# fp16 parts and a bound in place of fp32r in a feed-forward layer, with sums of squares for maxima

## The chip, the cores and the metric

The kernel runs on one core of one Trainium2 chip. The core has TensorE (PE, with its weight loads shown as PEld), VectorE (DVE), ScalarE (ACT), GpSimd (POOL) and SyncE (SP, which issues most DMAs). The metric is device time in microseconds (us); lower is better. A profile is one further execution, recorded by the hardware profiler.

## What is computed

Attention over 4 batches, 12 heads, 448 positions, head size 64, with a mix of the heads before and after the softmax; its output is 1792 tokens of 768 values. Then two feed-forward layers:

```python
def _moe_ref(x, w_in, w_out):            # layer 0: d_ff 2048
    h = x @ w_in
    g = h * np.cos(h)
    return g @ w_out
def _moe2_ref(x, w_gate, w_val, w_out):  # layer 1: d_ff 1536
    g = x @ w_gate
    silu = g * (1.0 / (1.0 + np.exp(-g)))
    val = x @ w_val
    return silu * val @ w_out
```

The attention inputs are fp32; the weights `w_in`, `w_out`, `w_gate`, `w_val` and `w_out2` reach the kernel as fp64 words, of which it makes fp32 bits itself.

## The kernel before

**Order of the work.** Attention comes first (functions of `attention`, planned block by block, 180 blocks); during its last chunk `early_plan` places the first work of layer 0 among its blocks, at s plus a number, s being the first block of the last chunk. Then `run` and `steps` write out the order of the rest by hand: a list of steps (layer, group g of 256 hidden columns, token block t of 448 tokens), 8 groups x 4 blocks in layer 0 and 6 x 4 in layer 1. Step i does the first product (`l1`, L737 to L739) of entry i in two halves e, and the second product (`l2`, L840 to L842) of entry i - 1, output by output (m from 0 to 5). Each engine takes its instructions strictly in the order in which they are issued, so this order is the schedule.

**Precision by parts.** An operand is split into a high and a low part, and three matmuls (high x high, high x low, low x high) stand for one in fp32. The first products of both layers use fp16 parts, with the weights scaled by a power of two, found from their maxima. In layer 0 the second product uses parts in fp32r, both for the activation (`hidden_b`, L783 and L784) and for `w_out`, which therefore needs no scale; in layer 1 it uses fp16 parts: `hidden_b`, `hidden_c` and `hidden_d` find the maximum of each activation block (L775) and scale by it.

**One step of layer 0.** PE: 36 matmuls of the first product and 36 of the second, each 128 x 128 weights by 448 columns. DVE per half: L759 and L760 (the angle of the cosine), then, after ACT's Sin (L761), L771, the product with the hidden value. ACT casts it to the high part, POOL subtracts for the low part. For each of the six outputs DVE adds the PSUM result to the accumulator in SBUF (`l2`, L850; group 0 is a copy by ACT, L846). The second product has three PSUM banks, the first four.

**Weights.** `load_next` issues the DMA of one raw half slab (384 KB) from SP into one of 8 buffers (`RAWS`). `w_max` (L517, DVE) takes the maximum of a half; `w_sum` (L526 to L531) joins those of a batch and makes a power of two; `w_sum_all` (L539) is a matmul with ones over the partitions; `w_unit` (L547, L548) gives the scale and its inverse. A half is converted by `w_shift` (ACT, L559), three bit operations (`w_bits`, L567, L569, L573, DVE), and `w_split` (ACT cast L597, POOL subtraction L598); `w_by` (L608) makes the product of the scales. `w_steps` lists this work: three items for a conversion (one for each bit operation, with what belongs to it), one item for a maximum; the maxima of a batch are put ahead of the conversion before. `fill(n)` takes the next n items, where their room (the earliest step) is reached and no sum is pending. In a step of layer 0 the calls are: `fill(3)` before the first half, one after its angle, one after its product, and three during the second product.

**From layer 0 to layer 1.** In the last group each finished output of `l2` gets a maximum by DVE (L854), six for a token block; `next_max` and `next_unit` make a scale of them; `next_part` writes layer 1's input parts: for the last three outputs and for block 0, ACT scales (L884) and casts (L885) and POOL subtracts (L886).

Of the kernel before, what the change touches and what calls it, by code (L numbers as in the profile page):

```python
# [46 lines left out]
RAWS = 8  # L47
# [3 lines left out]
def f(ap):  # L51
    return ap.bitcast(F32)
# [386 lines left out]
class FeedForward:  # L439


    def __init__(self, ctx, tc, xs, w_in, w_out, w_gate, w_val, w_out2, outT):
        self.ctx, self.tc, self.xs, self.outT = ctx, tc, xs, outT
        self.X, self.raw, self.part, self.G, self.W, self.PH = {}, {}, {}, {}, {}, {}
        self.n_ps = self.n_wi = 0
# [5 lines left out]
        self.unit = [self.p_const.tile([128, 4], F32, name=f"unit{layer}") for layer in range(2)]  # L451
        self.scale, self.by = {}, {}
        self.hm = {}
# [11 lines left out]
    def open_early(self):  # L465
        self.p_wr = self.pool("m_wr", RAWS, side="right")
# [14 lines left out]
    def open_late(self):  # L481
        self.p_wo = self.pool("m_wo", 4)
        self.p_wi.append(self.pool("m_wi1", WI - 2))
# [28 lines left out]
    def w_max(self, key, z):  # L512


        u, i = self.scale[key]
# [5 lines left out]
    def w_sum(self, batch):  # L521

        nc = self.tc.nc
        u = self.scale[batch[0]][0]
        m = u[:, 2]
        nc.vector.tensor_tensor(m, u[:, 0], u[:, 1], op=ALU.max)  # L526
        if batch[0][1] == "o":
            nc.vector.tensor_tensor(m[:, 0:1], m[:, 0:1], m[:, 1:2], op=ALU.max)
            nc.vector.tensor_copy(m[:, 1:2], m[:, 0:1])
        nc.vector.tensor_scalar(m, m, 2.0 ** -112, None, op0=ALU.mult)  # L530
        nc.vector.tensor_scalar(  # L531
            m.bitcast(I32), m.bitcast(I32), 3, 0x7C000000, op0=ALU.logical_shift_left, op1=ALU.bitwise_and
        )

    def w_sum_all(self, batch):

        ps = self.part["sum", batch[0]] = self.ps_sum("su_" + self.nm(batch[0], 0))
        m = self.scale[batch[0]][0][:, 2].bitcast(BF16)[:, 1::2]
        self.tc.nc.tensor.matmul(ps[:, 0:2], self.ones, m, start=True, stop=True)  # L539

    def w_unit(self, batch):
# [3 lines left out]
        u = self.scale[batch[0]][0].bitcast(I32)  # L545
        ps = self.part.pop(("sum", batch[0]))[:, 0:2].bitcast(I32)
        nc.vector.tensor_scalar(u[:, 3], ps, 0x7C000000, None, op0=ALU.bitwise_and)  # L547
        nc.vector.tensor_scalar(  # L548
            u[:, 4], u[:, 3], 3, 31 << 23, op0=ALU.logical_shift_right, op1=ALU.bitwise_xor
        )  # L550

    def w_shift(self, key, z):
# [4 lines left out]
        t = self.p_wr.tile([128, 3, 128], F32, tag="f", bufs=2, name="f_" + self.nm(key, z))  # L557
        by = self.one(key, 4) if key in self.scale else 2.0 ** -112
        nc.scalar.activation(t, top, AF.Copy, scale=by)  # L559
# [18 lines left out]
    def one(self, key, row):  # L578
        u, i = self.scale[key]
        return u[:, row, i:i + 1]  # L580

    def w_split(self, key, z):
        nc = self.tc.nc
        first, half = key[1] == "i", key in self.scale
# [478 lines left out]
```

## Time and profile before

| | |
|---|---|
| median of 3 runs | 1395.35 us (1393.73 to 1397.68) |
| profiled execution | 1398.5 us, span on the core 1396.7 us |
| PE busy | 1366.9 us (98%), 9580 matmuls |
| PE weight loads | 883.6 us (63%) |
| DVE busy | 1050.7 us (75%), 2416 instructions |
| ACT busy | 649.2 us (46%) |
| POOL busy | 444.8 us (32%) |
| HBM read and written | 75.45 and 10.37 MB |

Layer 0 runs from about 430 to 915 us of the span, layer 1 from there to the end. A row of a group (by line) has the line, engine and operation, output and input tiles, shapes, count; then busy us and the mean ns of one; then the idle time of the engine just ahead of these instructions and what ended it. A row of a timeline has start, duration, engine, line, operation, tiles and, in brackets, the idle time before it and what it waited for. Matmuls are pipelined: the profile's duration of one is longer than the distance to the next.

### The profile page before, as it was taken

The numbers are of one execution on the slowest core, as the hardware profiler recorded it, in microseconds if no ns is written. First come the engines' busy times: TensorE is split into PE (matmuls) and PEld (weight loads), VectorE is DVE, ScalarE is ACT, GpSimd is POOL, SyncE is SP. The second block draws the span as 40 slices with busy tenths as digits, with TensorE's granted clock in tenths as the row PEclk, the third lists the DMA queues.
The fourth block names the chain that finished last, engine by engine and source line by source line (L and its number), as shares of the span: only waits on it lengthen the run. The fifth ranks groups of instructions, "written<-read, shape, count | busy, mean of one in ns | idle before, by whom it ended". The sixth has DMA issues, their size and how long they took to land.

```text
span 1396.7 us, 25451 instructions
## 1 busy us (share of the span) xinstructions
PE 1366.9 (98%) x9580; PEld 883.6 (63%) x9580; DVE 1050.7 (75%) x2416; ACT 649.2 (46%) x1360; POOL 444.8 (32%) x499
## 2 busy tenths in 40 slices
PE   6999999999999999999999999999999999999998
PEld 3677776777766767777777777655555555555554
DVE  5888978888877768887888889886676757666334
ACT  3677677686765543243333332556432333233121
POOL 3353344353323333233333332433231222223010
PEclk8999999999999999999999999999999999999999
DMA  5555465555474221122222121112221112110012
GB/s 187 161 154 156 132 172 147 137 163 163 112 231 142 62 75 57 57 71 62 61 69 68 57 59 56 46 46 70 67 80 56 58 49 76 46 46 1 0 47 112
DMA packets 100211, 126.17 MB, mean 90 GB/s; under 512 B 29592, under 2 KB 88440, under 8 KB 100088
## 3 DMA queue, kind: packets, MB, share of 16 engines
q1 hardware_dynamic: 99248, 123.26, 30.0%
q8 instruction: 75, 1.23, 0.4%
q10 hardware_dynamic: 840, 1.29, 0.3%
q14 instruction: 48, 0.39, 0.1%
HBM read 75.45 MB, written 10.37 MB: 61 GB/s over the span
## 4 chain that ended last, share of the span: by engine, by line
PE 83%; DVE 8%; ACT 3%; DMA 2%; issue 2%; POOL 1%; ACTq 0%; SPq 0%; POOLq 0%; DVEq 0%
PE ph L737 11%; PE ph L738 11%; PE ph L739 11%; PE psm L238 9%; PE py L840 9%; PE py L841 8%; PE py L842 8%; PE psv L312 4%; PE pss L213 4%; PE psa L287 3%; PE psa L288 2%; PE psa L289 2%; DVE mx L854 1%; DVE el L274 1%; DMA x<-s 1%
## 5 line engine op out<-in xcount | busy, mean ns | idle before, releaser
L737 PE MATMUL ph<-x,h_i 128*128 128x448 f16 x960 | 338.4, 353 | 0.0
L738 PE MATMUL ph<-x,h_i 128*128 128x448 f16 x960 | 338.3, 352 | 0.2 <-POOL x L886 0.2
L739 PE MATMUL ph<-x,l_i 128*128 128x448 f16 x960 | 338.3, 352 | 0.0
L840 PE MATMUL py<-gh,h_o 128*128 128x448 f32 (+1 forms) x672 | 247.7, 369 | 3.6 <-DVE acc L850 2.5
L841 PE MATMUL py<-gl,h_o 128*128 128x448 f32 (+1 forms) x672 | 241.9, 360 | 0.4 <-DVE gl L815 0.4
L842 PE MATMUL py<-gh,l_o 128*128 128x448 f32 (+1 forms) x672 | 241.0, 359 | 0.0
L267 POOL TENSOR_SCALAR eh<-e,sm 120x448 f16<-120x448 f32 x180 | 115.4, 650 | 216.6 <-DVE sm L258 96.7
L238 PE MATMUL psm<-x,wpre_sb 120*120 120x448 f32 x360 | 160.1, 568 | 6.8 <-DMA x<-s 3.5
L251 ACT ACTIVATE e<-psm,sm 120x448 f32<-120x448 f32 x180 | 113.6, 636 | 85.0 <-DVE sm L243 67.1
L737 PEld LDWEIGHTS <-h_i 128*128 128x128 f16 x960 | 93.8, 98 | 89.7 <-issue 5.2
L739 PEld LDWEIGHTS <-l_i 128*128 128x128 f16 x960 | 93.8, 98 | 88.4 <-issue 0.4
L738 PEld LDWEIGHTS <-h_i 128*128 128x128 f16 x960 | 93.9, 98 | 80.9
L598 POOL TENSOR_TENSOR l_i<-f_i,h_i 128x384 f16<-128x384 f32 x80 | 76.0, 950 | 216.5 <-ACT h_i L597 201.5
L243 DVE TENSOR_REDUCE sm<-psm 120x1 f32<-120x448 f32 x180 | 108.7, 619 | 44.3 <-PE psm L238 37.7
L848 DVE SCALAR_TENSOR_TENSOR acc<-py,hm,acc 128x448 f32<-128x448 f32 x120 | 79.2, 678 | 82.3 <-PE py L842 81.4
L771 DVE SCALAR_TENSOR_TENSOR r<-ph,by_i,r 128x448 f32<-128x448 f32 x112 | 76.3, 681 | 70.3 <-ACT r L764 55.0
L784 POOL TENSOR_TENSOR gl<-r,gh 128x448 fp32r<-128x448 f32 x64 | 77.7, 1214 | 150.1 <-ACT gh L783 146.4
L274 DVE SCALAR_TENSOR_TENSOR el<-e,sm,eh 120x448 f16<-120x448 f32 x180 | 124.1, 730 | 0.7 <-POOL eh L267 0.5
L287 PE MATMUL psa<-wpost,eh 120*112 120x120 f16 x720 | 121.4, 219 | 2.3 <-ACT at L301 2.3
L289 PE MATMUL psa<-wpost,el 120*112 120x120 f16 x720 | 119.8, 217 | 0.0
L288 PE MATMUL psa<-wpost,eh 120*112 120x120 f16 x720 | 119.8, 217 | 0.0
L850 DVE TENSOR_TENSOR acc<-py,acc 128x448 f32<-128x448 f32 x168 | 103.2, 618 | 14.8 <-PE py L842 11.2
(130 smaller groups left out, 2361.9 us busy)
## 6 DMA issues: line engine op xcount, KB each, us to landing
r_o<-in_w_out SPq DMA_DIRECT2D x56, 384.0 KB
x<-s SPq DMA_DIRECT2D x84, 210.0 KB
r_i<-in_w_in SPq DMA_DIRECT2D x32, 384.0 KB
x<-s SPq DMA_DIRECT2D x48, 192.5 KB
r_i<-in_w_gate SPq DMA_DIRECT2D x24, 384.0 KB
r_i<-in_w_val SPq DMA_DIRECT2D x24, 384.0 KB
x<-s SPq DMA_DIRECT2D x48, 175.0 KB
qr<-in_qT SPq DMA_DIRECT2D x15, 360.0 KB
```

What stands on the lines that cost most here:

```text
L238: nc.tensor.matmul(ps[:120, :S], wpre_sb, X[b, c][:120, k], start=True, stop=True)
L267: nc.gpsimd.tensor_scalar(eh, E[b, c, k], sm[:, 3:4], 1.0, op0=ALU.mult, op1=ALU.mult)
L274: nc.vector.scalar_tensor_tensor(el, E.pop((b, c, k)), sm[:, 3:4], eh, op0=ALU.mult, op1=ALU.subtract)
L287: nc.tensor.matmul(o, eh[:, j], wpost_sb[0], start=True, stop=False)
L288: nc.tensor.matmul(o, eh[:, j], wpost_sb[1], start=False, stop=False)
L289: nc.tensor.matmul(o, el[:, j], wpost_sb[0], start=False, stop=True)
L737: nc.tensor.matmul(ps, wh, xh, start=(kk == 0), stop=False)
L738: nc.tensor.matmul(ps, wh, xl, start=False, stop=False)
L739: nc.tensor.matmul(ps, wl, xh, start=False, stop=(kk == 5))
L840: nc.tensor.matmul(ps, wh, gh[:, e], start=(e == 0), stop=False)
L841: nc.tensor.matmul(ps, wh, gl[:, e], start=False, stop=False)
L842: nc.tensor.matmul(ps, wl, gh[:, e], start=False, stop=(e == 1))
```

## The change

Layer 0's activation parts `gh`, `gl` and the parts of its `w_out` become fp16. `w_out`'s scale comes from its maxima, which makes four more `w_max` and a `w_sum`, `w_sum_all` and `w_unit` for each group of layer 0. The activation's scale is no maximum: its size is bounded by that of the first product, so a second, finer power of two is formed along with the first weights' scale (`w_sum` with mask `FINE`, three more operations in `w_unit`), and `hidden_b` multiplies by it (`fine`). One scale now serves both halves of a layer 0 group, so `w_by` runs once for the two. `y_by0` makes the factor by which a group's second product is added, and `l2` accumulates by a scalar_tensor_tensor with it (ACT with that scale for group 0). `y_by0` also adds these factors up to a bound on the output (`total`); in the last group ACT squares each finished output, scaled by the bound's inverse, with a sum over the columns, in place of DVE's maximum; the square's own output goes to a dead part of `X[t]`; `next_unit` takes a square root of a power of two by a shift. Raw weights have 8 + 4 buffers, the four opened at the end of attention, with four more loads there. The first `fill` of a layer 0 step takes 4 items for 3; the conversion of the first second weights in `early_plan` moves from s + 13 to s + 16, behind their new maxima and sum.

```diff
-RAWS = 8
+COARSE, FINE, EVEN = 0x7C000000, 0x7FFF0000, 0x7F000000
+RAWS = 8, 4
+OUTS = 13, 15, 16, 16, 17
...
     def w_dma(self, key, z):
...
-        raw = self.p_wr.tile([128, 3, 128], I64, tag="raw", name="r_" + self.nm(key, z))
+        late = len(self.p_wr) > 1 and self.n_raw % sum(RAWS) < RAWS[1]
+        self.n_raw += len(self.p_wr) > 1
+        raw = self.p_wr[late].tile([128, 3, 128], I64, tag="raw", name="r_" + self.nm(key, z))
...
     def w_sum(self, batch):
...
+        u, _, _, n = self.scale[batch[0]]
+        m = u[:, 0, :n]
+        nc.vector.tensor_tensor(u[:, 0], u[:, 0], u[:, 1], op=ALU.max)
+        if n == 1:
+            nc.vector.tensor_tensor(m, m, u[:, 0, 1:2], op=ALU.max)
         nc.vector.tensor_scalar(m, m, 2.0 ** -112, None, op0=ALU.mult)
+        for k, mask in ((1, FINE), (0, COARSE))[batch[0][:2] != (0, "i"):]:
+            nc.vector.tensor_scalar(
+                (u[:, 0, 1:2] if k else m).bitcast(I32), m.bitcast(I32), 3, mask,
+                op0=ALU.logical_shift_left, op1=ALU.bitwise_and,
+            )
...
     def w_unit(self, batch):
...
+        nc.vector.tensor_scalar(u[:, 2, :n], ps[:, :n], COARSE, None, op0=ALU.bitwise_and)
+            u[:, 3, :n], u[:, 2, :n], 3, 31 << 23, op0=ALU.logical_shift_right, op1=ALU.bitwise_xor
+        if batch[0][:2] == (0, "i"):
+            up, down = f32[:, 2, 1:2], f32[:, 3, 1:2]
+            nc.vector.tensor_scalar(up.bitcast(I32), ps[:, 1:2], EVEN, None, op0=ALU.bitwise_and)
+            nc.vector.tensor_scalar(down.bitcast(I32), up.bitcast(I32), EVEN, None, op0=ALU.bitwise_xor)
+            nc.vector.tensor_scalar(down, down, f32[:, 2, 0:1], 2.0 ** -5, op0=ALU.mult, op1=ALU.mult)
...
+    def y_by0(self, key):
+        g = key[2] // 2
+        d = self.d[g] = self.by[0, "i", 0, 2 * g][:, 0]
+        nc, total = self.tc.nc, self.total
+        nc.vector.tensor_scalar(d, d, self.one(key, 2), None, op0=ALU.mult)
+        if g == 0:
+            nc.vector.tensor_copy(total[:, 0], d)
+            return
+        nc.vector.tensor_tensor(total[:, 0], total[:, 0], d, op=ALU.add)
+        if g == FF1 // 256 - 1:
+            nc.vector.tensor_scalar(total[:, 0], total[:, 0], 2.0 ** 33, 2.0 ** -100, op0=ALU.mult, op1=ALU.max)
+            nc.vector.reciprocal(total[:, 1], total[:, 0])
...
     def hidden_b(self, layer, g, t, e):
...
+        if layer == 0:
+            by = self.fine(g, 3)
+        else:
+            by = self.by[1, "i", 1, 2 * g + e][:, 0, t:t + 1]
...
     def l2(self, layer, g, t, m):
...
-        if g == 0 and layer == 1:
+        if g == 0:
             nc.scalar.activation(acc, ps, AF.Copy, scale=d)
-        elif g == 0:
-            nc.scalar.copy(acc, ps)
-        elif layer == 1:
+        else:
             nc.vector.scalar_tensor_tensor(acc, ps, d, acc, op0=ALU.mult, op1=ALU.add)
-        else:
-            nc.vector.tensor_tensor(acc, ps, acc, op=ALU.add)
         if last and layer == 0:
...
-            nc.vector.tensor_reduce(
-                out=self.mx[t][:, m:m + 1], in_=acc, axis=AX.X, op=ALU.max, apply_absolute_value=True
+            nc.scalar.activation(
+                self.X[t][1][:, m].bitcast(BF16), acc, AF.Square, scale=self.total[:, 1, t:t + 1],
+                accum_out=self.mx[t][:, m:m + 1],
             )
...
     def early_plan(self, s):
...
-            plan.append((s + 13 + j, self.w_shift, *key))
-            plan.append((s + 14 + j, self.w_bits, *key))
+            plan.append((s + OUTS[3] + j, self.w_shift, *key))
+            plan.append((s + OUTS[4] + j, self.w_bits, *key))
+        rows = self.rows(0, 0)
+        plan.append((s, self.new_scale, rows))
+        for j in range(4):
+            plan.append((s + OUTS[0] + j // 2, self.w_max, rows[j % 2], j // 2))
+        for d, step in enumerate((self.w_sum, self.w_sum_all, self.w_unit)):
+            plan.append((s + OUTS[1] + (d > 0) * (OUTS[2] - OUTS[1]), step, rows))
...
     def steps(self):
...
+        for j in range(RAWS[1]):
+            self.load_next()
...
-                self.fill((3 + (i < 4), 5)[L])
+                self.fill((4, 5)[L])
```

## Rows read from the trace of the kernel before

**Rows 1.** chain that ended last, shares by engine (page, part 4)
```profile
PE 83%; DVE 8%; ACT 3%; DMA 2%; issue 2%; POOL 1%; ACTq 0%; SPq 0%; POOLq 0%; DVEq 0%
```

**Rows 2.** busy us of PE, PEld, DVE, ACT, POOL, clock, DMA by stretch
```profile
560.00:800.00 240.00, 240.00 (x1228) 172.73 (x1227) 199.53 (x383) 81.44 (x145) 78.29 (x73) 1.00 0.22 63
880.00:895.00 15.00, 13.17 (x66) 9.20 (x65) 13.77 (x34) 10.85 (x19) 9.42 (x9) 1.00 0.09 28
920.00:960.00 40.00, 38.95 (x210) 19.90 (x209) 30.79 (x75) 30.18 (x56) 16.54 (x17) 1.00 0.25 74
```

**Rows 3.** groups of PE instructions by line and shape, whole span
```profile
L840 PE MATMUL py<-gh,h_o 128*128 128x448 f32 x384 | 146.2, 381 | 2.7 <-DVE acc L850 2.5 <-ACT acc L846 0.2
L840 PE MATMUL py<-gh,h_o 128*128 128x448 f16 x288 | 101.4, 352 | 0.9 <-ACT acc L844 0.9
```

**Rows 4.** timeline of PE, start us, us, line, operation, tiles
```profile
600.17 0.36 PE L840 MATMUL py<-gh,h_o 128*128 128x448 f32 x1
...
602.59 0.36 PE L840 MATMUL py<-gh,h_o 128*128 128x448 f32 x1
603.24 0.35 PE L737 MATMUL ph<-x,h_i 128*128 128x448 f16 x1
...
609.67 0.35 PE L738 MATMUL ph<-x,h_i 128*128 128x448 f16 x1
```

**Rows 5.** timeline of PE, first second-product matmul of four steps
```profile
468.15 0.53 PE L840 MATMUL py<-gh,h_o 128*128 128x448 f32 x1
...
850.32 0.53 PE L840 MATMUL py<-gh,h_o 128*128 128x448 f32 x1
...
865.47 0.53 PE L840 MATMUL py<-gh,h_o 128*128 128x448 f32 x1
...
880.05 0.53 PE L840 MATMUL py<-gh,h_o 128*128 128x448 f32 x1
```

**Rows 6.** groups by line, accumulations on DVE in layers 0 and 1
```profile
L850 DVE TENSOR_TENSOR acc<-py,acc 128x448 f32<-128x448 f32 x168 | 103.2, 618 | 14.8 <-PE py L842 11.2 <-PE su_i L539 1.6
L848 DVE SCALAR_TENSOR_TENSOR acc<-py,hm,acc 128x448 f32<-128x448 f32 x120 | 79.2, 678 | 82.3 <-PE py L842 81.4
```

**Rows 7.** timeline of DVE
```profile
693.97 0.68 DVE L771 SCALAR_TENSOR_TENSOR r<-ph,by_i,r 128x448 f32<-128x448 f32 x1 [0.27 <-ACT r L761]
...
876.77 1.46 DVE L517 TENSOR_REDUCE u_i<-r_i 128x1 f32<-128x384 f32 x3
878.26 0.16 DVE L526 TENSOR_TENSOR u_i<-u_i 128x2 f32<-128x2 f32 x1
878.46 0.17 DVE L530 TENSOR_SCALAR u_i<-u_i 128x2 f32<-128x2 f32 x1
```

**Rows 8.** groups by line, whole span, tiny operations on DVE
```profile
L531 DVE TENSOR_SCALAR u_i<-u_i 128x2 int32<-128x2 int32 x20 | 6.1, 306 | 0.7
L794 DVE TENSOR_SCALAR hm<-hm 128x1 int32<-128x1 int32 x24 | 3.7, 154 | 0.8
```

**Rows 9.** timeline of ACT, two Exp with accumulator, one after the other
```profile
428.05 0.63 ACT L251 ACTIVATE e<-psm,sm 120x448 f32<-120x448 f32 x1 [1.43 <-DVE sm L243]
...
428.67 0.62 ACT L251 ACTIVATE e<-psm,sm 120x448 f32<-120x448 f32 x1
```

**Rows 10.** timelines of POOL and PE at layer 1's first product
```profile
891.90 1.04 POOL L886 TENSOR_TENSOR x<-nx,x 128x448 f16<-128x448 f32 x1 [0.20 <-ACT x L885]
...
893.18 0.35 PE L738 MATMUL ph<-x,h_i 128*128 128x448 f16 x1
```

**Rows 11.** waits of PE in total, times, longest
```profile
PE su_i L539 <- DVE u_i L531: 3.0, 1, 3.0
```

**Rows 12.** maxima of layer 1's second weights by line; the chain at 936 us
```profile
L517 DVE TENSOR_REDUCE u_o<-r_o 128x1 f32<-128x384 f32 x24 | 12.2, 544 | 4.5 <-DMA r_o<-in_w_out 4.5
...
936.24 3.06 DMA r_o<-in_w_out
```

**Rows 13.** groups by line, ACT's table loads, the last of three
```profile
L764 ACT ACT_TABLE_LOAD x1 | 1.3, 1283 | 0.0
```

More of the change, by code (lines that the diff above doesn't have):

```diff
@@ L556, in w_shift @@
         top = self.raw[key, z].bitcast(F32).rearrange("p m (n w) -> p m n w", w=2)[:, :, :, 1]
-        t = self.p_wr.tile([128, 3, 128], F32, tag="f", bufs=2, name="f_" + self.nm(key, z))
-        by = self.one(key, 4) if key in self.scale else 2.0 ** -112
-        nc.scalar.activation(t, top, AF.Copy, scale=by)
+        t = self.p_wr[0].tile([128, 3, 128], F32, tag="f", bufs=2, name="f_" + self.nm(key, z))
+        nc.scalar.activation(t, top, AF.Copy, scale=self.one(key, 3))
         self.part[key, z] = t
@@ L578, in one, with fine @@
     def one(self, key, row):
-        u, i = self.scale[key]
+        u, _, i, _ = self.scale[key]
         return u[:, row, i:i + 1]
+    def fine(self, g, row):
+        return self.scale[0, "i", 0, 2 * g][0][:, row, 1:2]
     def w_split(self, key, z):
         nc = self.tc.nc
-        first, half = key[1] == "i", key in self.scale
+        first = key[1] == "i"
         tag = self.slab(key)[1]
@@ L588, in w_split @@
             self.n_wi += first
-            shape, dt = ([128, 6, 128], F16 if first else F32R) if first or not half else ([128, 12, 128], F16)
             self.W[key] = tuple(
-                pool.tile(shape, dt, tag=tag + p, name=p + "_" + self.nm(key, z))[:, :6] for p in "hl"
+                pool.tile([128, 6, 128], F16, tag=tag + p, name=p + "_" + self.nm(key, z)) for p in "hl"
             )
-            if first and (key[0] == 0 or key[3] > 3):
+            if first and (key[0] == 0 and key[3] % 2 == 0 or key[3] > 3 and key[0] == 1):
                 self.w_by(key)
+            if key[0] == 0 and not first and key[2] % 2 == 0:
+                self.y_by0(key)
         hi, lo = (w[:, 3 * z:3 * z + 3] for w in self.W[key])
@@ L607, in w_by @@
         for i, c in enumerate((0.5, 0.5 * INV2PI) if layer == 0 else (0.5,)):
+            own = self.one(key, 2)
+            if layer == 0 and i == 0:
+                own, c = self.fine(key[3] // 2, 2), 8.0
             nc.vector.tensor_scalar(
-                self.by[key][:, i, ts], self.unit[layer][:, ts], self.one(key, 3), c,
-                op0=ALU.mult, op1=ALU.mult,
-            )
+                self.by[key][:, i, ts], self.unit[layer][:, ts], own, c, op0=ALU.mult, op1=ALU.mult
+            )
+    def y_by0(self, key):
[10 more added lines that the diff above has]
+            nc.vector.reciprocal(total[:, 1], total[:, 0])
     def batches(self, layer, g):
@@ L623, in new_scale @@
     def new_scale(self, batch):
-        u = self.p_unit.tile([128, 5, 2], F32, tag="u", bufs=6, name="u_" + self.nm(batch[0], 0))
+        u = self.p_unit.tile([128, 4, 2], F32, tag="u", bufs=11, name="u_" + self.nm(batch[0], 0))
+        one = batch[0][0] == 0 or batch[0][1] == "o"
         for i, key in enumerate(batch):
-            self.scale[key] = u, i
+            self.scale[key] = u, i, 0 if one else i, 1 if one else 2
     def w_steps(self):
@@ L639, in w_steps @@
                 if bi == 0 and n > 1:
-                    rows = self.rows(*groups[n - 1]) if groups[n - 1][0] else None
-                    convs.append((rows, outs(*groups[n - 1]), 4 * (n - 2) + 1, ("o", *groups[n - 1])))
+                    convs.append((self.rows(*groups[n - 1]), outs(*groups[n - 1]), 4 * (n - 2) + 1, ("o", *groups[n - 1])))
                 if batch:
@@ L748, in hidden_a @@
         if e == 0:
-            shape, dt = (([128, 2, S], F32R), ([128, 4, S], F16))[layer]
             self.G[g, t] = tuple(
-                self.p_g.tile(shape, dt, tag=f"g{p}", name=f"g{p}{layer}_{g}_{t}")[:, :2] for p in "hl"
+                self.p_g.tile([128, 2, S], F16, tag=f"g{p}", name=f"g{p}{layer}_{g}_{t}") for p in "hl"
             )
```

51 lines of the change are left out of this document (22 added, 29 removed).

## The prediction, made before the changed kernel ran

> **What bounds the kernel now.** I read the chain of waits first: TensorE (PE) holds 83% of the chain that ends last, VectorE (DVE) 8% [rows 1]. Then the busy time by stretch: in a quiet part of layer 0, from 560 to 800 us, PE is busy in all of the 240 us at a granted clock of 1.00 (2.4 GHz, the upper level), DVE in 199.53, ScalarE (ACT) in 81.44, GpSimd (POOL) in 78.29 [rows 2]. So in the stage that the change rewrites, time falls only if PE's instructions come closer together, and DVE, 83% busy, must follow.
>
> How close they come is read from starts in the PE timeline, since the matmul durations overlap. From 600.17 to 602.59 there are 12 steps between fp32r matmuls of the second product: 201.7 ns each. From 603.24 to 609.67 there are 34 steps between fp16 matmuls of the first product: 189.1 ns [rows 4]. The fp16 second product of layer 1 has a mean of 352 ns against 381 in fp32r [rows 3]; its shape is that of layer 0's fp16 matmuls, so I give it 189.1 too. A saving of 12.6 ns lies on the path. A (group, token block) step has 36 matmuls of each product, so PE needs 36 x (201.7 + 189.1) = 14.07 us. The second products of steps 2 and 29 begin at 468.15 and 850.32 [rows 5]: 27 steps of 14.15. After the change PE alone needs 72 x 189.1 = 13.62, plus some 0.02 for small sum matmuls: 13.64.
>
> **The change part by part.** *PE, steps 1 to 32.* 36 x 12.6 ns = 0.454 us a step, 14.5 us over all 32: the ceiling of what fp16 gives. Steps 1 to 4 have conversions held back by pending sums, so DVE has room there: 4 x 0.454 = **-1.8 us**.
>
> *DVE in steps 5 to 28.* It is busy 199.53/240 x 14.15 = 11.76 us a step now. Added:
> - the six accumulations become scalar_tensor_tensor, 678 ns for 618 [rows 6]: 0.36 us;
> - the list of conversion work grows from 28 to 32 items a group, and the fills from 8 to 9 a step. Three maxima take 1.46 us back to back [rows 7]: one more item 0.49 us;
> - tiny operations: 9 a group before (three in the sum, two in the unit, four scale products); 20 after (five and five for the first weights, two products, four and two for the second weights, two for the activation's scale). At 3.5 and 3.56 steps a group that is 2.6 and 5.6 a step. Two successive ones start 0.20 us apart [rows 7]: 3.0 x 0.20 = 0.60 us.
>
> Sum 13.21. DVE also waits 0.27 us a step for ACT's Sin in the first half [rows 7]; nothing in the change fills that. So 13.48 us of DVE against 13.64 of PE: PE still leads, by a hair, and DVE has nothing to catch up with after a late accumulation. With three PSUM banks for the second product, PE stops when an accumulation is over two banks late. Now, at 83%, the mean step loses 0.08 (14.15 - 14.07). With no slack I put the loss between 0 and 0.49 (one item late each step) and take 0.16, nearer what the trace has: a step of 13.80. 24 x (14.15 - 13.80) = **-8.4 us**.
>
> Here a small cost decides. The 128x2 tensor_scalar of L531 has a mean of 306 ns [rows 8] though an undisturbed operation of two columns takes 0.17 us [rows 7], while the 128x1 ones of L794 have a mean of 154 over 24 [rows 8]. The change makes layer 0's sums one element wide, so I price no such wait. The Trainium skill, SBUF — State Buffer, "Who interferes with whom", says that a DVE tensor_scalar can take a port pair that it shares with GpSimd, and that a running holder then blocks the other wholly. The 306 agrees; the 154 does not, for single elements.
>
> Off the path: casts of activation and weights to fp16 in place of fp32r keep their element counts; ACT's accumulation of group 0 and shifts with a scale pointer cost some 0.1 us each on an engine that is busy 34% [rows 2]; if that cover were gone, Sin would come late and DVE with it. POOL's subtractions, 33%, are no longer than now.
>
> *Layer switch, steps 29 to 32.* 24 maxima of the accumulator leave DVE. Steps 29 and 30 now last 15.15 and 14.58 [rows 5], with DVE the late engine: 1.00 + 0.43 over the mean 14.15 returns, -1.4. PE's own 0.454 counts for three of the four steps, -1.4. The maxima become ACT squares with a sum. The nearest row is the Exp with its accumulator read, whose successor starts 0.62 later [rows 9]. In step 31 ACT is busy 10.85 of 15 us [rows 2] and makes layer 1's first inputs; four squares, each behind its accumulation, now stand ahead of the last three of them: 4 x 0.62 = 2.5 us late. The last low part ends at 891.90 + 1.04 = 892.94 and its matmul starts at 893.18 [rows 10]: 0.24 of slack, so about 2.3 of new wait, of which I take 2.0 (bounds 0, if ACT's gaps hold the squares, and 7.4, all twelve squares of steps 31 and 32 exposed). Together **-0.8**. Its sum matmul and next scale have a step of time, free.
>
> *Ramp.* PE stands 3.0 us for the first sum [rows 11]; two more tiny operations go ahead of that: +0.4. The four new maxima, 1.96 us, fall where DVE waits for ACT in the attention's tail; the second weights' shift moves back by three blocks, past other work of ACT, and may be late for the first second product: +0.3. Bounds of both: -0.4 (the moved shift frees ACT for as much) and +3.1 (one load waited for, [rows 12]). Four loads more go to SP's queue at the end of attention; what stands behind them is loads of later groups. **+0.7.**
>
> *Raw buffers.* In layer 1 the maxima of the second weights wait 4.5 us for loads, one piece of 3.06 on the chain [rows 12]. Twelve buffers issue a load four halves earlier. PE is busy 38.95 of the 40 us around there [rows 2], so 1.05 is all that can return: **-0.3** (0 to -1.05).
>
> Sum: -1.8 - 8.4 - 0.8 + 0.7 - 0.3 = -10.6. The profiled execution took 1398.5 us (its span is 1396.7), 3.15 over the median of 1395.35; 1398.5 becomes 1387.9, and the median **1384.8 us**. Its own range, with the bounds of the step loss (13.64 to 14.0) and the switch: 1381 to 1390.
>
> **The rivals.**
> - *DVE stays wholly hidden*: steps of 13.64, squares in ACT's gaps, no ramp cost: -1.8 - 12.2 - 2.8 - 0.3 = -17.1, **1378.2**. For: 13.48 is below 13.64, and PE was never idle from 560 to 800. Against: 99% of use in a queue in order.
> - *The squares take the place of the reductions*: all twelve beside layer 1's inputs exposed, 7.4 for 2.0, +5.4: **1390.2**. For: the 0.24 of slack. Against: step 32 has more room than step 31.
> - *Tiny operations wait for POOL*: each of the 3.0 added ones meets a running POOL operation with POOL's share, 0.33, and waits half of 1.04 [rows 2, 10]: 0.17 x 3.0 = 0.51. DVE needs 13.99, with the 0.16 a step of 14.15: the 8.4 is gone, **1393.2**. For: the 306 of L531 [rows 8]. Against: L794. The page of the Trainium skill named above would have it so for every tensor_scalar that meets its conditions.
> - *Slower: the second weights' maxima wait for their loads in layer 0 as well.* DVE takes its queue in order; a maximum that waits holds up accumulations, and PE with them. Price: 3.06 a group as in layer 1 [rows 12], seven groups, 21.4: 1384.8 + 21.4 = **1406.2**. It eats the gain from 1.5 us a group, and is slower by 0.3% from 2.1. Against: with twelve buffers the halves of a maximum were issued twelve items, about 1.3 steps or 18 us, earlier.
> - *The square needs a table of its own*: now three loads in the whole run, 1283 ns each [rows 13]. Squares stand between Sin and Silu in four steps; four loads a step is 20 us of ACT, perhaps half exposed: +10, **1394.8**. Against: copies between the same functions cause no load. That fp16 would not speed the second product is excluded by layer 1's rows [rows 3].
>
> **How the numbers follow.** Forecast 0.47, hidden DVE 0.20, squares 0.10, POOL 0.08, loads 0.11, table 0.04. A measurement here can tell about 0.3%, 4.2 us, from no change: faster means under 1391.2. Faster: 0.47 + 0.20 + 0.06 of the squares = 0.73; slower: the loads and 0.01 of the table, 0.12; the rest, 0.15, is the same. The range 1378 to 1396 takes in all but the loads and the tails.
>
> **What would show it.** Right: starts of the second product's matmuls in layer 0 at 189 ns; steps of 13.7 to 13.9; DVE at 95% or more there; PE waits on the accumulation of some 0.1 to 0.2 a step; an ACT row of 24 squares of about 0.65 with no table load beside them; no reduction of the accumulator on DVE; a PE wait of about 2 us for POOL's low part at the first product of layer 1. Wrong: matmul starts that stay at 202 ns; DVE under 90% with steps of 13.64 (hidden); maxima that wait for DMA in layer 0 (loads); tensor_scalar of one element with means near 0.3 us (POOL).

## The result, and the profile of the changed kernel

The changed kernel takes 1384.28 us (median of 6 runs, 1382.54 to 1386.28) against 1396.78 for the kernel before beside it: a ratio of 0.9914, 95% interval 0.9901 to 0.9928. That is faster by more than the 0.3% that can be told here, and 0.5 us from the 1384.8 forecast. The profiled execution took 1383.52 us with a span of 1381.7, 15.0 less than the span before. How far the terms of the sum agree is read from the starts of the second products in the timeline of PE, in us:

| stretch | before | changed | difference | forecast |
|---|---|---|---|---|
| span's start to the first second product | 456.75 | 453.97 | -2.78 | +0.7 (ramp) |
| steps 1 to 4 | 53.89 | 53.24 | -0.65 | -1.8 |
| steps 5 to 28 | 339.68 | 332.23 | -7.45 | -8.4 |
| steps 29 and 30 | 29.73 | 27.29 | -2.44 | -0.8 for 29 to 32 |
| steps 31 and 32 | 45.38 | 44.80 | -0.58 | |
| steps 33 and 34 | 42.51 | 41.55 | -0.96 | -0.3 |
| the rest | 428.76 | 428.62 | -0.14 | 0 |

The first line is not the change's: PE's first psv matmul in the attention already starts 3.2 us earlier (61.17 for 64.38), and over the kernels below the first second product began anywhere from 452.60 to 458.99. Counted from that psv matmul, the first second product comes 0.4 us later (392.79 for 392.37). The runs below whose ramp is the changed kernel's have 391.3 to 393.2 there, so the ramp's own cost is not resolved within about 1 us.

The chain's shares and the windows that answer to [rows 1, 2]. In a window line the columns are its ends, its length, busy us of PE, PEld, DVE, ACT and POOL with their instructions, clock, DMA share, GB/s:

```profile
PE 85%; DVE 9%; ACT 2%; DMA 2%; issue 1%; POOL 0%; SPq 0%; DVEq 0%; POOLq 0%; ACTq 0%
```
```profile
560.00:800.00 240.00, 237.56 (x1261) 122.37 (x1259) 221.88 (x461) 84.97 (x148) 73.91 (x75) 1.00 0.23 65
860.00:880.00 20.00, 17.55 (x92) 8.65 (x91) 17.40 (x38) 16.26 (x36) 9.97 (x9) 1.00 0.13 39
920.00:960.00 40.00, 40.00 (x217) 20.73 (x216) 25.29 (x61) 26.88 (x48) 14.45 (x14) 1.00 0.25 70
```

DVE went from 199.53 to 221.88 us in the quiet stretch of layer 0, and PE, never idle there before, now stands 2.4 us. From 920 to 960 PE has lost its gap.

The groups that answer to [rows 3, 6, 8, 12, 13] and to the estimate from [rows 9], by line and shape (busy us, mean ns of one | idle before it):

```profile
L872 PE MATMUL py<-gh,h_o 128*128 128x448 f16 x672 | 236.7, 352 | 5.4 <-DVE acc L878 3.3 <-ACT acc L876 1.9
L878 DVE SCALAR_TENSOR_TENSOR acc<-py,by_i,acc 128x448 f32<-128x448 f32 x168 | 110.1, 675 | 7.0 <-PE py L874 5.6 <-PE su_o L546 0.7 <-PE su_i L546 0.7
L882 ACT ACTIVATE x<-acc,total 128x448 bf16<-128x448 f32 x24 | 15.9, 663 | 6.1 <-DVE acc L878 6.0
L882 ACT ACTIVATION_READ_ACCUMULATOR x<-acc,total 128x1 f32 x24 | 4.5, 187 | 0.0
L523 DVE TENSOR_REDUCE u_o<-r_o 128x1 f32<-128x384 f32 x56 | 28.8, 542 | 0.0
L556 DVE TENSOR_SCALAR u_i<-u_i 128x2 int32<-128x2 int32 x12 | 2.9, 246 | 0.4
L636 DVE TENSOR_SCALAR by_i<-by_i,u_o 128x4 f32<-128x4 f32 x8 | 2.6, 319 | 0.0
L535 DVE TENSOR_SCALAR u_o<-u_o 128x1 f32<-128x1 f32 x14 | 2.2, 154 | 0.5
L640 DVE TENSOR_TENSOR total<-total,by_i 128x4 f32<-128x4 f32 x7 | 1.8, 257 | 0.2
L795 ACT ACT_TABLE_LOAD x1 | 1.3, 1283 | 0.0
```

All 672 second-product matmuls of a kind have the fp16 row's 352 ns. In a step without waits their starts lie 189.3 ns apart, 29 distances from the first to the last of these:

```profile
590.51 0.35 PE L872 MATMUL py<-gh,h_o 128*128 128x448 f16 x1
...
596.00 0.35 PE L874 MATMUL py<-gh,l_o 128*128 128x448 f16 x1
```

The 24 squares cost 663 ns and 187 for reading the sum, which overlap: two in a row start 0.65 us apart (at 871.14 and 871.79). They have no table load of their own. No maximum of a second weight waits for a load any more. The one-element operations of L535 stay at 154 ns. The means of the wider ones hide single long ones: of the eight of L636 one takes 1.00 us and the others 0.22, of the seven of L640 one takes 0.83 and the others 0.16.

The waits of PE in total (us, times, longest), as [rows 11], and the timeline's waits at the first product of layer 1, where [rows 10] had none:

```profile
PE su_i L546 <- DVE u_i L537: 3.4, 1, 3.4
PE py L872 <- DVE acc L878: 3.3, 6, 1.2
PE ph L770 <- POOL x L919: 2.6, 3, 1.1
PE py L872 <- ACT acc L876: 1.9, 4, 0.8
```
```profile
876.57 0.35 PE L769 MATMUL ph<-x,h_i 128*128 128x448 f16 x1 [0.17 <-ACT x L918]
877.99 0.35 PE L770 MATMUL ph<-x,h_i 128*128 128x448 f16 x1 [1.07 <-POOL x L919]
879.89 0.35 PE L770 MATMUL ph<-x,h_i 128*128 128x448 f16 x1 [1.15 <-POOL x L919]
```

Steps 5 to 28 are not evenly 13.84 us long: 16 of the 24 take 13.62 to 13.65, TensorE's pace, and eight take 13.84 to 14.96. A late one, from the timelines of PE and of DVE:

```profile
534.48 0.35 PE L872 MATMUL py<-gh,h_o 128*128 128x448 f16 x1
...
540.93 0.35 PE L872 MATMUL py<-gh,h_o 128*128 128x448 f16 x1 [0.61 <-DVE acc L878]
...
548.87 0.35 PE L872 MATMUL py<-gh,h_o 128*128 128x448 f16 x1
```
```profile
537.72 0.67 DVE L878 SCALAR_TENSOR_TENSOR acc<-py,by_i,acc 128x448 f32<-128x448 f32 x1
538.31 0.54 DVE L523 TENSOR_REDUCE u_i<-r_i 128x1 f32<-128x384 f32 x1
538.88 0.65 DVE L532 TENSOR_TENSOR u_i<-u_i 128x2 f32<-128x2 f32 x1
539.56 0.16 DVE L534 TENSOR_TENSOR u_i<-u_i 128x1 f32<-128x1 f32 x1
539.75 0.15 DVE L535 TENSOR_SCALAR u_i<-u_i 128x1 f32<-128x1 f32 x1
539.94 0.34 DVE L537 TENSOR_SCALAR u_i<-u_i 128x1 int32<-128x1 int32 x2
540.20 1.27 DVE L878 SCALAR_TENSOR_TENSOR acc<-py,by_i,acc 128x448 f32<-128x448 f32 x2
```

Between two accumulations stand the group's last maximum and the five operations of its sum, 1.9 us; PE has meanwhile filled its three banks. Of the 1.9, some 0.5 is in L532, which takes 0.65 us where the others of its line and shape, but for two, take 0.16. POOL runs a subtraction at that time, and L532 ends 0.02 us behind it (539.53 and 539.50). In another late step a bit operation of the conversion takes 1.36 us for its usual 0.55, again with POOL at work:

```profile
538.47 1.03 POOL L818 TENSOR_TENSOR gl<-r,gh 128x448 f16<-128x448 f32 x1 [2.54 <-ACT gh L817]
```
```profile
774.57 1.36 DVE L585 SCALAR_TENSOR_TENSOR f_i<-r_i,f_i 128x384 int32<-128x384 int32 x1
```
```profile
774.48 1.03 POOL L818 TENSOR_TENSOR gl<-r,gh 128x448 f16<-128x448 f32 x1 [2.69 <-ACT gh L817]
```

### The profile page after: what moved, and what is told of

Read it like the earlier page. It is cut to its first block, busy times and chain, and to the rows that moved or that the text cites. A ratio compares the mean times of both kernels' runs of the same rounds, so it can differ in the third digit from the quotient of the medians.

```text
span 1381.7 us, 25565 instructions
## 1 busy us (share of the span) xinstructions
PE 1348.0 (98%) x9588; PEld 783.0 (57%) x9588; DVE 1066.6 (77%) x2508; ACT 670.0 (48%) x1408; POOL 437.1 (32%) x499
## 4 chain that ended last, share of the span: by engine, by line
PE 85%; DVE 9%; ACT 2%; DMA 2%; issue 1%; POOL 0%; SPq 0%; DVEq 0%; POOLq 0%; ACTq 0%
PE ph L769 12%; PE ph L771 12%; PE ph L770 12%; PE psm L240 10%; PE py L872 8%; PE py L874 8%; PE py L873 8%; PE psv L314 5%; PE pss L215 5%; PE psa L289 3%; PE psa L291 2%; PE psa L290 2%; DVE acc L878 1%; DVE r L791 1%; DVE k L790 1%; DVE r L805 1%
## 5 line engine op out<-in xcount | busy, mean ns | idle before, releaser
L872 PE MATMUL py<-gh,h_o 128*128 128x448 f16 x672 | 236.7, 352 | 5.4 <-DVE acc L878 3.3
L873 PE MATMUL py<-gl,h_o 128*128 128x448 f16 x672 | 236.8, 352 | 0.3 <-DVE gl L849 0.3
L874 PE MATMUL py<-gh,l_o 128*128 128x448 f16 x672 | 236.8, 352 | 0.0
L818 POOL TENSOR_TENSOR gl<-r,gh 128x448 f16<-128x448 f32 x64 | 69.4, 1085 | 145.9 <-ACT gh L817 133.3
L878 DVE SCALAR_TENSOR_TENSOR acc<-py,by_i,acc 128x448 f32<-128x448 f32 x168 | 110.1, 675 | 7.0 <-PE py L874 5.6
L289 PEld LDWEIGHTS <-eh 120*112 120x112 f16 x720 | 94.1, 131 | 22.8 <-issue 18.0
```

What stands on the lines that cost most here:

```text
L289: nc.tensor.matmul(o, eh[:, j], wpost_sb[0], start=True, stop=False)
L872: nc.tensor.matmul(ps, wh, gh[:, e], start=(e == 0), stop=False)
L873: nc.tensor.matmul(ps, wh, gl[:, e], start=False, stop=False)
L874: nc.tensor.matmul(ps, wl, gh[:, e], start=False, stop=(e == 1))
L878: nc.vector.scalar_tensor_tensor(acc, ps, d, acc, op0=ALU.mult, op1=ALU.add)
```

## The experiments

### What fp16 alone gives

The kernel before with fp16 tiles for layer 0's hidden parts and second weights. The scaling is left out, so the low parts lose bits.

```
-  shape, dt = ([128, 6, 128], F16 if first else F32R) if first or not half else ([128, 12, 128], F16)
+  shape, dt = [128, 6 if first or key[0] == 0 else 12, 128], F16
-  shape, dt = (([128, 2, S], F32R), ([128, 4, S], F16))[layer]
+  shape, dt = [128, 4, S], F16
```

> The kernel before with layer 0's second product in fp16 and nothing else: no scales, so neither the extra maxima and one-element operations nor the scaled accumulation, the maxima of the next inputs stay on DVE, eight raw buffers. Left out: the scaling of hidden and second weights, so their low fp16 parts lose bits. Theory (the gain is TensorE's pace, 36 second-product matmuls at 189 instead of 202 ns, and what stayed behind of it are DVE operations that the change adds): steps 5 to 28 at 13.64 us, hardly any wait for acc, 24 x 0.51 = 12.3 us gained there, 1.8 in steps 1 to 4, about 0.9 in steps 29 and 30, whose stalls stay; with the two last second products of layer 0 some 16 us, ratio 0.988 to before, 3 to 5 us faster than the changed kernel. Rival (DVE was the pace before already, fp16 alone buys little): steps 5 to 28 stay near 13.9 to 14.1, gain under 7 us, ratio over 0.995. Rival (the steps of 13.84 to 14.96 are an inheritance of the order and not of the added operations): mean step 13.84, ratio 0.991.

1383.69 us, ratio 0.9902 (0.9889 to 0.9916): as fast as the whole change, within what can be told. Steps 1 to 4 take 51.66 us, -2.23; steps 5 to 28 328.30, a mean of 13.68, -11.4; steps 29 and 30 keep their stalls, 14.82 and 14.58. The gain is TensorE's pace, as the theory has it. The run was to be 3 to 5 us faster than the changed kernel, and wasn't: what the scaling costs before step 29 (1.6 + 3.9 us by the two traces) the rest of the change earns back behind it (2.1 us in steps 29 and 30, 1.7 in 31 and 32, 1.2 in 33 and 34). Most of the 1.7 is the clock in this run's step 31, told in the last section.

### The second weights without their own scale

The changed kernel with a constant for their scale, so no maxima, sums and units of them in layer 0, and three fills a step. The scaled accumulation stays. Left out: that scale.

```
-  convs.append((self.rows(*groups[n - 1]), outs(...), ...))
+  convs.append((self.rows(*groups[n - 1]) if groups[n - 1][0] else None, outs(...), ...))
-  scale=self.one(key, 3))
+  scale=self.one(key, 3) if key in self.scale else 2.0 ** -112)
-  self.fill((4, 5)[L])
+  self.fill((3 + (i < 4), 5)[L])
```

> The changed kernel without the scale of layer 0's second weights: no maxima of them, no sums and units, a constant in their place (the second weights are cast unscaled, their low parts lose bits), three fills a step as before; the scaled accumulation and the total stay. Theory (late steps come from the maxima and the clusters of tiny operations, 0.53 + about 0.4 us of DVE a step, and the scaled accumulation's 0.36 us a step fit under TensorE): steps 5 to 28 all near 13.64, mean under 13.70, so 3.5 to 5 us faster than the changed kernel, ratio to before 0.988. Rival (the accumulation in the second product's time is what makes them late): mean stays 13.80 to 13.85, time within 1 us of the changed kernel's. Rival (what is late is the fewer or more weight steps in the l2 phase): in between, and the late steps fall where three fills stand.

1378.49 us, ratio 0.987 (0.9854 to 0.9885), 5.8 us under the changed kernel. One of the 24 steps is late (14.06), the mean 13.65, which makes 4.7 us; steps 1 to 4 take 51.27, 2.0 less. So the longer accumulation is hidden, and the late steps come with the maxima and their tiny operations. DVE's busy time from 560 to 800 us puts a size on each: 205.71 with fp16 alone, 211.23 here, 221.88 in the changed kernel.

### Load, or place in the queue?

First the load: the angle's whole turns move to ACT.

```
-  nc.vector.tensor_scalar(k, ps, turn, 0.25, op0=ALU.mult, op1=ALU.add)
+  nc.scalar.activation(k, ps, AF.Copy, bias=0.25, scale=turn)
```

> The changed kernel with the angle's whole turns (L790, 0.68 us, two a step) on ACT in place of DVE: 1.3 us a step less on DVE, as much more on ACT, which is busy 35% in steps 5 to 28. Theory (DVE's lateness in the second product): late steps go, mean of steps 5 to 28 13.64 to 13.68, 4 to 5 us faster than the changed kernel, ratio to before about 0.988. Rival (the late steps are a matter of the order in DVE's queue at that place, not of the load): nothing gained, since k stands ahead of the first product's end and the cluster stays ahead of acc: within 1 us. Rival (the extra hand-off DVE, ACT, DVE, ACT makes gh late): waits for gh at the second product, slower by 0.3 us a step, 7 us.

1388.98 us, ratio 0.9938 (0.9926 to 0.995). DVE is busy 195.91 us from 560 to 800, less than in the kernel before, and yet the mean step is 14.00. Less load did not help, and no wait for gh appears, the last rival's sign. A line of DVE's timeline shows what the run brought along; the cluster of 538.88 stands behind it as it did:

```profile
535.23 0.68 DVE L791 SCALAR_TENSOR_TENSOR r<-ph,by_i,k 128x448 f32<-128x448 f32 x1 [0.70 <-ACT k L790]
...
538.64 0.65 DVE L532 TENSOR_TENSOR u_i<-u_i 128x2 f32<-128x2 f32 x1
```

DVE now stands at the angle until ACT has delivered, and the accumulations behind it stand with it. As this wait is new, the run can't say alone what the load does in the changed kernel.

Then the place, with the load unchanged: the sums go behind the next step's first weight steps, the units (and so PE's sum matmul) between its two first products.

```
+  def sum_parts(self): ... self.w_sum(...)
   self.fill((4, 5)[L])
+  self.sum_parts()
   ...
   self.hidden_b(L, g, t, 1)
-  self.sum_up()
+  if L:
+      self.sum_up()
```

> The changed kernel with the same instructions, but in layer 0 the sums (four or five tiny operations behind the fourth maximum) and the units (two or five behind PE's sum) are issued in the first product's time only: the sums behind the step's first four weight steps, the units between the two first products; 24 maxima and all else stay where they were. Theory (a late step comes from where a cluster of tiny operations stands in DVE's queue, ahead of acc in the second product, not from DVE's load): late steps mostly go, mean of steps 5 to 28 under 13.70, 3 to 5 us faster than the changed kernel, with the same DVE busy time. Rival (DVE's load of 92.5% with maxima inside the second product is what matters): mean stays over 13.80, within 1 us. Rival (the later sums make PE wait for su or hold up the weight steps): waits for su_i of 0.5 us and more, or steps over 14 us at the group's ends.

1400.06 us, ratio 1.0026 (1.0016 to 1.0035): slower than the kernel before. The rival on PE's side came in, as the waits of PE show, one line from the whole span and two from the timeline:

```profile
PE su_i L546 <- DVE u_i L537: 7.4, 6, 3.4
PE su_o L546 <- DVE u_i L561: 5.4, 1, 5.4
```
```profile
468.17 0.19 PE L546 MATMUL su_o<-u_o,ones 128*128 128x2 bf16 x1 [5.39 <-DVE u_i L561]
...
557.16 0.18 PE L546 MATMUL su_i<-u_i,ones 128*128 128x2 bf16 x1 [1.21 <-DVE u_i L537]
```

A sum matmul that follows its operand by a few operations holds up everything in PE's queue. One wait of 5.4 us falls in step 1; in steps 5 to 28, 6.0 us longer than in the changed kernel, the waits for sums are 6.4 us, and those for acc are left in two steps only. With the squares' order below added to it:

> The changed kernel with both: tiny sums and units of layer 0 in the first product's time, and squares of tokens 2 and 3 behind the parts of x. Theory (two separate places, so the gains add): 3 to 5 us from steps 5 to 28 and 2.5 us at the layer switch, 5.5 to 7.5 us faster than the changed kernel, ratio to before 0.986 to 0.987. Rival (one takes the other's gain back): no faster than the better of the two alone.

1397.31 us, ratio 1.0014 (1.0002 to 1.0025): the same loss in layer 0, and steps 31 to 33 shorter than in the run before it by 0.85 us in all.

The third try keeps PE's sums half a step behind. What a weight step brings of tiny operations during a second product is held until its last accumulation is issued, and the unit goes to the next place outside the second product.

```
+  def after_acc(self, fn, *a): held.append((fn, a)) if hold else fn(*a)
-  (self.w_sum, what), (self.add_sum, what)
+  (self.add_sum, what)     # w_sum through after_acc
-  self.y_by0(key)
+  self.after_acc(self.y_by0, key)
   ...
+  self.release()           # behind l2's six columns
   self.sum_up()
```

> The changed kernel with the same instructions, but what a weight step of layer 0 brings along of tiny operations during a second product (sums, by, total) is issued behind the step's last acc, and the units at the next of the two places outside the second product; maxima and bit steps stay inside, PE's sums keep at least half a step behind DVE's. Theory (a cluster of tiny operations ahead of acc in DVE's queue makes a step late, and the run that moved the sums failed by PE's waits for them alone): no late step over 14.0 from step 5 to 28, mean 13.65 to 13.72, no waits for su, 3 to 4.5 us faster than the changed kernel. Rival (three maxima or bit steps of 0.55 us inside the second product are enough to make it late): mean 13.78 or more, within 1.5 us. Rival (every move of the sums makes PE wait for them): waits for su of 0.5 us and more, slower.

1382.67 us, ratio 0.9896 (0.988 to 0.9913), and in the trace:

```profile
560.00:800.00 240.00, 239.84 (x1277) 123.97 (x1275) 222.92 (x467) 86.58 (x151) 75.90 (x76) 1.00 0.23 66
```

DVE is as busy as in the changed kernel (222.92 for 221.88), PE stands 0.16 us there instead of 2.44, two steps are late (14.95, 14.05) and the mean is 13.71: 3.3 us less in steps 5 to 28. That shows it: the same operations made steps late by where they stood. The lateness of step 7 only moved into step 8 (28.77 us for the two before, 28.59 now); the gain is in steps 15 to 24. The median gained 1.6 only, less than the 3 to 4.5 expected; 1.67 of the profiled run's time went in step 31, by the clock (0.65 from 876 to 880 us; see the last section).

What makes a place late is not taken apart. In seven of the changed kernel's eight late steps a DVE operation meets a running subtraction of POOL, just ahead of the accumulations or between them, and takes longer than others of its form: by 0.3 us in steps 8 and 15, 0.5 in 7 and 23, 0.8 in 24 and 25, 1.4 by two operations in 18. That is some 4.6 us beside the 4.9 that steps 5 to 28 take above 24 x 13.64. In the held run only step 25's is left of these, and step 8 has another, of 0.6 us near its start. Other meetings cost nothing: 0.3 us some 4 us into steps 6, 17, 22 and 27, 0.5 us at 5.7 us into step 13, 0.6 us at 9 to 10 us into steps 6, 11, 22 and 27, none of them late. So whether the row of operations or the meeting with POOL counts for more at the bad place is open; no run moved one without the other.

### The layer switch

The squares of tokens 2 and 3 wait until the parts of layer 1's first x are issued.

```
-  nc.scalar.activation(..., AF.Square, ...)
+  self.squares.append((t, m))
   ...
+  if m > 2 or not 0 <= t_new < 4:
+      self.square()
```

> The changed kernel with the squares of tokens 2 and 3 held back until the second product's fourth column, behind the parts of layer 1's first x. Theory (the wait at the layer switch is ACT's queue, a square of 0.76 us between any two parts of x): the two PE waits for POOL's x of 1.07 and 1.15 us and the later one of 0.38 go, step 31 from 23.75 to about 21.7, 2 us faster than the changed kernel. Rival (POOL's own 1.0 to 1.4 us for a low part sets them): waits stay over 1.5 us, nothing gained. Rival (the held back squares make the next unit late): a wait for sx or ACT x in the next step takes back 1 us or more.

1381.37 us, ratio 0.9889 (0.9873 to 0.9904). Step 31 falls from 23.75 to 21.15, step 32 rises by 0.67, and of the waits for x one is left, 0.3 us. So ACT's queue set them, and POOL's own time, still over 1.0 us for a low part, did not. (From a square's start to the end of its sum's reading is 0.75 us, but the next instruction starts 0.65 to 0.67 us behind the square's start.)

And the squares themselves undone, with the maxima back on DVE:

```
-  nc.scalar.activation(..., AF.Square, ..., accum_out=self.mx[t][:, m:m + 1])
+  nc.vector.tensor_reduce(out=self.mx[t][:, m:m + 1], in_=acc, axis=AX.X, op=ALU.max, apply_absolute_value=True)
```

> The changed kernel with the next inputs' maxima back on DVE (24 of 0.62 us) in place of ACT's squares, and the unit taken from them as in the kernel before. Theory (the squares take DVE's load off steps 29 and 30 and cost a wait for layer 1's x): steps 29 and 30 go from 13.65 and 13.64 to about 14.8 and 14.6, as in the run with fp16 alone, the waits for POOL's x of 2.6 us shrink and a wait for acc takes their place; step 31 24 to 25.4; in all 2 to 4 us slower than the changed kernel. Rival (the squares only move the wait): steps 29 and 30 lose 2 us, step 31 gains 2 us, within 1 us of the changed kernel. Rival (the squares hurt, as their queue delays x): 2 us faster.

1390.2 us, ratio 0.9956 (0.9944 to 0.9968): 5.9 us slower than the changed kernel, more than expected. Steps 29 to 34 take 14.94, 15.52, 24.75, 22.54, 21.84 and 20.48 us, together 6.4 more, and the waits for acc are where the time goes:

```profile
PE py L872 <- DVE acc L878: 9.7, 12, 1.6
```

### The raw buffers

Eight raw buffers in the changed kernel (RAWS = 8, 0):

> The changed kernel with the eight raw buffers of before in place of twelve. Theory (the wait for a raw second weight in layer 1 was worth about 1 us, and layer 0's maxima of second weights are early enough even with eight): steps 5 to 28 stay at a mean of 13.84, DVE waits for a raw o tile of some us come back after 920 us and PE's stretch 920 to 960 falls from 40.0 to about 39 us busy; 0.5 to 1.5 us slower than the changed kernel. Rival (with maxima a group earlier, eight buffers make layer 0's maxima wait for their loads): waits for DMA in DVE's queue in steps 5 to 28, mean step 14.0 to 14.5, 5 to 20 us slower. Rival (buffers don't matter): same time, no DMA waits.

1384.4 us, ratio 0.9918 (0.9905 to 0.9931), no difference. Layer 0 is the same to 0.04 us, so the rival's price is not paid: DVE's maxima of first weights do wait for loads there, 1.88 us in step 3, 0.13 in step 10 and 0.24 in step 26, without making a step longer. In layer 1 the maxima of second weights wait again, but from 1068 us on, and PE is busy in all 40.00 us from 920 to 960:

```profile
L523 DVE TENSOR_REDUCE u_o<-r_o 128x1 f32<-128x384 f32 x56 | 29.0, 544 | 3.6 <-DMA r_o<-in_w_out 3.6
```

The other way round, twelve buffers added to fp16 alone:

> The kernel with fp16 alone, and of the rest of the change only the twelve raw buffers with their four earlier loads. Left out as there: the scaling of hidden and second weights. Theory (the two steps after the layer switch, 21.36 us each with fp16 alone and 21.07 and 20.48 in the changed kernel, are late by the loads of raw second weights, which twelve buffers bring forward): the two steps fall to 41.0 to 41.6 us together, DVE's wait of some 5 us for raw second weights goes, the run is 0.5 to 1.2 us faster than fp16 alone. Rival (those loads cost nothing there, and the two steps are late through ACT's and DVE's queues at the switch, which other parts of the change emptied): DVE's waits for loads go, the two steps stay at 42.3 to 42.8 us together, the same time as fp16 alone.

1382.91 us, ratio 0.9897 (0.988 to 0.9913). The 5.7 us of waits for raw second weights are gone, and the two steps take 21.35 and 20.67 us: 0.70 of the 1.17 looked for, between both expectations. So the buffers are worth 0.7 us where nothing else was changed, and nothing where the rest was; which other part does the same work is open.

### The two reorderings together

> The run before this one together with the squares of tokens 2 and 3 behind the parts of x. Theory: the gains add, 2.5 us at the layer switch and 3 to 4.5 in steps 5 to 28: 5.5 to 7 us faster than the changed kernel, ratio to before 0.987. Rival (the switch's gain depends on where the late tiny operations stand): less than 1.5 us faster than the run with the tiny operations alone.

1378.41 us, ratio 0.9867 (0.9853 to 0.9882), the fastest kernel that computes the whole: 5.9 us under the changed one, and as fast as the run that leaves the second weights' scale out. Steps 5 to 28 are at 13.71, step 31 at 21.15. One weight step moved on from the second product to the front of the step, as a last try:

> The run before this one, with the weight step of the second product's fourth column moved ahead of the first product (five there in place of four) in layer 0. Theory (what is left of lateness is weight steps between the accs): steps 5 to 28 all at 13.62 to 13.66, up to 1 us faster than the run before this one. Rival (five steps ahead of the angle make gh late): waits for gh, slower by 1 to 5 us.

1383.4 us, ratio 0.9903 (0.9888 to 0.9917), 5.0 us slower than the run before it. Nine steps are late (13.71 to 15.34), which costs 2.5 us; another 2.2 are lost in steps 31 and 32, where PE waits for acc 0.76, 0.37 and 1.94 us. In all PE waited 5.5 us for acc, and for gh not at all, so it is not the rival as stated: around the late accumulation at 610 us DVE works without a gap from the angle on. Which of the moved operations made that so was not taken apart.

## Why the forecast held, point by point

**The pace.** 12.6 ns a matmul, 36 a step, was right: steps come to 13.62 to 13.65 wherever DVE is in time, as forecast (13.64), and fp16 alone gives 11.4 us in steps 5 to 28.

**DVE's load.** 199.53 became 221.88; by steps that is 221.88/240 x 13.84 = 12.80 us where the sum said 13.21, so PE's lead over DVE's work is 0.8 us and not 0.4, and with the wait for Sin (0.28 measured, for 0.27) it is 0.6, not "a hair"; DVE is busy 92% of the time where the forecast looked for 95% or more. The base was right (205.71/240 x 13.68 = 11.73 with fp16 alone, for 11.76); the added 1.45 measured 1.07. The accumulation, 6 x (675 - 618) ns = 0.34 for 0.36, was close; the remaining 0.7, for 1.09, was priced too high, partly because 0.2 us from start to start counts gaps that busy time does not.

**The step loss** of 0.16, "nearer what the trace has", measured 0.20, and gave 7.45 us for 8.4. The size held, its mechanism did not. The forecast let DVE's lack of slack lose a little in every step; two thirds of the steps lose nothing, and the run with the same load and another order wins back 3.3 of the 4.9 us. The step that failed is the one from busy time to lateness: a queue in order is late by what stands ahead of the awaited instruction, and by what that in turn waits for.

**Tiny operations and POOL.** One-element tensor_scalars do not wait, 149 to 154 ns in the rows of L535, L537, L555 and L556, as priced. A one-element tensor_tensor can: L534 takes 0.90 us for 0.16 once in the run without the second weights' scale (at 485.64). The 306 ns of L531, on which the forecast weighed this rival, is no usual time: in the kernel before 17 of the 20 take 0.17 us and three take 1.08, and those three stand in steps 7, 14 and 21, three of the four that were late there. The 128x4 ones, put at 0.20 with the rest, take 0.22 and 0.16 but for one of each, and these two stand where it matters. DVE and POOL in the latest step of all (14.96):

```profile
690.90 1.00 DVE L636 TENSOR_SCALAR by_i<-by_i,u_o 128x4 f32<-128x4 f32 x1
691.94 0.83 DVE L640 TENSOR_TENSOR total<-total,by_i 128x4 f32<-128x4 f32 x1
```
```profile
690.60 1.28 POOL L818 TENSOR_TENSOR gl<-r,gh 128x448 f16<-128x448 f32 x1 [2.07 <-ACT gh L817]
691.84 0.90 POOL L614 TENSOR_TENSOR l_o<-f_o,h_o 128x384 f16<-128x384 f32 x1
```

Each ends when POOL's does: 691.90 beside 691.88, 692.77 beside 692.74. PE then waits 1.16 us at 693.41. The Trainium skill, SBUF — State Buffer, "Who interferes with whom", has this wait both for a tensor_scalar and for a DVE instruction with two SBUF inputs beside a GpSimd one that reads SBUF; the second half, which the forecast passed over, agrees here with L640 and with L532 at 538.88. So the rival's waits do come, in few places and not in each step, and with those of the bit operations some 4.6 us of them stand in late steps.

**The ramp and steps 1 to 4.** -1.1 together; -0.65 measured in steps 1 to 4, and a ramp near +0.4 that is not resolved. Fp16 alone has -2.23 in steps 1 to 4, the change -0.65: the second weights' four maxima stand in DVE's queue at 461.51 for 1.92 us, ahead of step 2's angle, ACT's accumulation of group 0 starts late behind it, and PE waits 0.77 us at 469.52 in a step of 14.80 us (14.25 before). Without these maxima step 2 takes 13.64 us and steps 1 to 4 51.27. The 1.8 took DVE's room there for granted. The first sum's wait went from 3.0 to 3.4, as forecast.

**The layer switch.** -0.8 forecast, -3.0 measured: the term that was furthest off. Steps 29 and 30 gave back what was said (2.44, for 1.4 + 0.9). The new wait for x came, 0.17 + 1.07 + 1.15 = 2.4 for 2.0, with the place named. Left out was that DVE's maxima had cost in steps 31 and 32 too: the kernel before waits in step 31 1.40 us for acc at 888.23 and 0.42 for the maximum's sum at 890.13, in step 32 0.32 for acc at 910.45, and all three are gone. Undoing the squares costs 5.9 us; the forecast had them at a net loss of 0.6 (1.4 returned, 2.0 of new wait).

**Raw buffers.** -0.3, measured -0.96 in steps 33 and 34, within the bound of 1.05, though the eight-buffer run says that it wasn't the buffers here.

**The rivals.** DVE hidden: nearly so in 16 steps, not in the rest. Squares in place of the reductions: their wait is real, their net a gain. POOL: not for one-element tensor_scalars, yes for wider operations and those with two inputs in SBUF, in few steps and not in each. Loads, the slower side: no maximum of a second weight waits in layer 0, with eight buffers neither. A table for the square: three loads as before.

That the median came within 0.5 us is luck in part. The errors partly cancel: about 0.9 (with the unresolved ramp) and 1.0 us less gain than forecast in layer 0, 2.2 and 0.7 more behind it. And the kernel before, at 1395.35 in the runs that the forecast knew, has a median of 1396.78 over all six, so that the gain is 12.5 us where 10.6 was forecast.

## What to carry to other kernels

Before counting an engine's busy share, list what stands between two awaited instructions in its queue: here 1.9 us of small operations ahead of an accumulation, 0.5 of it a wait for POOL, made a step late, where 92% of busy time alone did not. A mean over such operations hides the few that wait; look at each one's time. A matmul that sums a statistic wanted its operand half a step earlier here, or PE stopped for it. And ask of a moved reduction what it was holding up in each of the steps where it stood, not only in the one with the visible stall.

## What was not expected of the hardware

With the same three waits for x, step 31 took 23.75 us in the changed kernel but 25.23 with eight buffers and 25.42 in the run of the held tiny operations. With fp16 alone, where step 31 has waits for acc instead, it was 25.40, and 23.78 when twelve buffers were added. The granted clock fell there in some executions and not in others. The changed kernel, and the one with eight buffers, in windows from 876 to 884 us, with a matmul of the latter's timeline behind PE's standing:

```profile
876.00:880.00 4.00, 1.61 (x7) 0.57 (x6) 2.88 (x7) 3.97 (x10) 2.76 (x2) 1.00 0.36 99
880.00:884.00 4.00, 4.00 (x22) 2.05 (x21) 0.92 (x2) 2.95 (x6) 2.19 (x2) 1.00 0.32 102
```
```profile
876.00:880.00 4.00, 2.18 (x7) 0.83 (x7) 1.59 (x2) 2.95 (x8) 2.94 (x3) 0.77 0.61 175
880.00:884.00 4.00, 4.00 (x18) 1.90 (x17) 0.92 (x2) 3.23 (x5) 1.28 (x1) 0.80 0.08 26
```
```profile
878.56 0.53 PE L770 MATMUL ph<-x,h_i 128*128 128x448 f16 x1 [1.15 <-POOL x L919]
878.89 0.58 PE L771 MATMUL ph<-x,l_i 128*128 128x448 f16 x1
879.26 0.58 PE L769 MATMUL ph<-x,h_i 128*128 128x448 f16 x1
```

Eight matmuls start 0.37 us apart instead of 0.19, the lower level of 1.2 GHz for the upper of 2.4, after PE's three waits of 2.4 us in all: 1.5 us more, so that the stall cost nearly 4. The four profiled runs with the squares held back show the clock at 1.00 there (868 to 892 us, and 886 to 910 in the one that runs later), so part of what that order gains in the medians may be this; how often the clock falls without it isn't settled by one profile a kernel.
